# Attention and two expert layers in one kernel: query and key loads moved in the attention's table, and layer 2's token sums in place and operand by operand

## The chip, the core and the metric

The kernel runs on one core of a Trainium2 chip. The core has a matrix engine (PE, with its weight loads shown as PEld), a vector engine (DVE), a scalar engine (ACT), a general one (POOL) and a queue engine (SP) that issues transfers to 16 DMA engines. Each engine takes its instructions in the order of its program and waits on semaphores for the others. The metric is the time of one execution on the device, in microseconds (us); the time given for the kernel before is the median of three runs.

## What is computed

Attention over 4 batches and 12 heads of 448 tokens with 64 numbers each, with queries and keys normalised by their root mean square; then two layers, each up, activation and down, on 1792 tokens of width 768 with 2048 hidden units.

```python
q_n, k_n = (rmsnorm(q, g_q), rmsnorm(k, g_k))
scores = scale * np.matmul(q_n, k_n.transpose(0, 1, 3, 2))
attn = np.exp(scores - max) ; attn = attn / (sum(attn) + 1e-09)
x = (attn @ v) as tokens x 768
h = x @ w_in ;  g = h * (1.0 / (1.0 + np.exp(-h))) ;  y = g @ w_out      # layer 1
h = y @ w_in2 ; g = np.maximum(h, 0.0) ** 2 ;         out = g @ w_out2   # layer 2
```

## The kernel before

**Number format.** Products are made of split operands: an upper part (hi) by a cast, L493 or L495, and a lower part (lo) by a subtraction, L502, and three products of parts per product. The four weight matrices come as 64-bit numbers; each unit of a weight (768 or 512 columns of 128 rows) is loaded raw (L846), turned into 32-bit by one ACT pass (L853) and DVE passes (L857, L861, L867, L873), stored for its later uses (L881, "keep", tiles ki, ko, kp, kq), and split (L493, L502). Later uses load it again (L833).

**Attention.** 24 pairs of heads follow one another. Of each pair, SP loads queries and keys (L516, tile qk, a ring of three buffers) and values (L633). ACT squares them (L527), DVE sums, POOL and DVE take the inverse root in small steps, POOL normalises (L589, two operations, after which the qk buffer is free), PE turns the tiles (L601). Then four chunks of scores follow (L654), each with the maximum on DVE (L665), the exponential on ACT (L672), and turning on PE (L681); PE multiplies with the values (L730), and ACT copies the result into xf (L481). The row sums of the exponentials are inverted, stored into DRAM (L709, tile rd) and read back spread over the partitions (L718, tile R, a ring of two). POOL multiplies xf by R (L753, the step "attended"), and the result is stored (L785, "keep_x", x) for the later batches, or split for layer 1 at once.

**Layers.** Layer 1 runs in 8 segments, 2 halves of the tokens by 4 quarters of the hidden units: up products (L954), silu in two steps (ACT L966, DVE L971), split into gg (one buffer), down products (L1008), sums (L1020); its result y is stored in DRAM (L1040). Layer 2 runs in two halves of 8 groups: each product of token blocks and weights in seven products (L1173, Strassen's scheme) instead of eight, so that it needs sums of weight blocks (L1141) and of token blocks, then relu squared (L1203 to L1207), the split into gh and gl, and the down products (L1249) that DVE adds up (L1276) and SP stores at the end of a half (L1290). The token blocks are made in `combine` (L1054 to L1113): per chunk of 128 rows it loads up to four blocks of y (L1074, tile yf, a ring of five), takes differences (L1084, the step "y_sum", function `less`), and splits them into the operands B11, T2, T3, T4 and, in a second group that may be done later, B21, T1, B22 (`put`).

**What sets the order.** All of it is written as steps of a plan (L97 to L357). A list scheduler with nominal durations simulates the five engines and issues each engine's steps in the order that it finds; buffers come from rings (L25), and a ring's next use waits for all users of the buffer. The steps of the attention are fixed (L141): they are taken on their engine in the order of their nominal times, which is the pair's number times 2 x 5.3 plus the entry of the table `nominal` (L50 to L64). Other steps fill the gaps if the plan finds that they fit before the next fixed step. A number of the table is thus an order, not a wait. The second pool of buffers, which holds gg and yf, opens only when the attention's own buffers are done with, the last keep_x among them (`swap_pools`, L1303).

## Time and profile before

| | |
|---|---|
| runs | 1266.6, 1271.03, 1272.84 us; median 1271.03 |
| the profiled execution | 1261.43 us, its span 1259.5 us |
| mean granted clock of PE | 0.987 |
| busy: PE, DVE, ACT, POOL | 1202.9 (96%), 939.1 (75%), 535.2 (42%), 238.9 us (19%) |
| attention | up to some 320 us of the span |
| layer 1 | some 320 to 790 us |
| layer 2, first and second half | some 790 to 1035 us, and to the end |

The span runs from the first to the last instruction; the profiled execution's time is 1.9 us longer. A timeline row gives the start, the duration, the engine, the line, and the tiles as out<-in; in square brackets stands how long the engine was idle ahead of it and what released it. PEclk is PE's granted clock as a share of 2.4 GHz. SPq is SP's queue of transfers.

### The profile page before, as it was taken

What the parts mean: (1) busy time and instruction counts of PE and PEld (TensorE: products, weight loads), DVE (VectorE), ACT (ScalarE), POOL (GpSimd) and SP (SyncE); (2) the same over time, 40 slices, a digit from 0 to 9 for tenths busy, and PEclk for the clock granted to TensorE, in tenths of its full rate; (3) what the DMA queues carried; (4) which work ended last, traced back from release to release, by engine and by line L of the source; (5) the groups of instructions that cost most, each with busy time, mean ns of one, the idle gap of its engine ahead of it and who ended that gap; (6) DMA issues with size and microseconds to landing.
All of it is one profiled execution on the core that took longest, in us unless ns stands there. A gap on an engine that the chain in (4) does not pass through costs nothing. (4 is left out here: it accounts for less than half of the span.)

```text
span 1259.5 us, 19054 instructions
## 1 busy us (share of the span) xinstructions
PE 1202.9 (96%) x6960; PEld 1050.1 (83%) x6960; DVE 939.1 (75%) x1624; ACT 535.2 (42%) x1129; POOL 238.9 (19%) x449
## 2 busy tenths in 40 slices
PE   5998999999999999999999999999999989999998
PEld 3665666666899999899999988899999988999998
DVE  6887978887588986989899878866667882555554
ACT  6887887776243231434333224443222433221111
POOL 6565656551100100101000001011111100000000
PEclk9998989999999999999999998999999999999999
DMA  5444445557565544597877846945555694544444
GB/s 160 81 98 104 83 90 100 87 101 106 159 184 154 172 130 147 166 339 222 242 253 230 253 160 214 346 170 205 219 211 189 231 310 180 173 169 158 138 141 135
DMA packets 134109, 220.75 MB, mean 175 GB/s; under 512 B 31104, under 2 KB 99456, under 8 KB 134016
## 3 DMA queue, kind: packets, MB, share of 16 engines
q1 hardware_dynamic: 134016, 219.54, 57.8%
q8 instruction: 55, 0.90, 0.4%
q14 instruction: 38, 0.31, 0.1%
HBM read 145.88 MB, written 73.62 MB: 174 GB/s over the span
## 5 line engine op out<-in xcount | busy, mean ns | idle before, releaser
L954 PE MATMUL t<-xb,w 128*128 128x448 f32 x1152 | 243.8, 369 | 6.7 <-DVE g L971 6.6
L1008 PE MATMUL s<-gg,w 128*128 128x448 f32 x1152 | 240.1, 365 | 1.3 <-DVE gg L502 1.3
L954 PEld LDWEIGHTS t<-xb,w 128*128 128x128 f32 x1152 | 217.8, 190 | 26.4 <-DVE g L971 8.2
L1008 PEld LDWEIGHTS s<-gg,w 128*128 128x128 f32 x1152 | 216.2, 188 | 19.0 <-DVE gg L502 1.8
L1249 PE MATMUL s<-w,gh 128*128 128x384 f32 x896 | 227.9, 335 | 0.0
L1249 PEld LDWEIGHTS s<-w,gh 128*128 128x128 f32 x896 | 162.4, 188 | 1.9 <-DVE gg L1276 0.3
L1249 PE MATMUL s<-w,gl 128*128 128x384 f32 x448 | 150.5, 336 | 6.0 <-DVE gl L502 5.9
L1276 DVE TENSOR_TENSOR gg<-s,gg 128x384 f32<-128x384 f32 x196 | 107.7, 554 | 55.4 <-PE s L1249 55.1
L672 ACT ACTIVATE E<-s,mx 112x448 f32<-112x448 f32 x192 | 121.1, 645 | 12.9 <-DVE mx L665 11.1
L1189 DVE TENSOR_TENSOR g<-t,g 128x448 f32<-128x448 f32 x96 | 58.2, 620 | 85.7 <-ACT g L481 57.3
L681 PEld LDWEIGHTS t<-ident,E 112*112 112x112 f32 x768 | 76.7, 138 | 52.5 <-ACT E L672 26.1
L681 PE MATMUL t<-ident,E 112*112 112x112 f32 x768 | 102.1, 274 | 15.9 <-ACT E L672 11.5
L665 DVE TENSOR_REDUCE mx<-s 112x1 f32<-112x448 f32 x192 | 110.8, 619 | 8.3 <-PE s L654 6.8
L502 POOL TENSOR_TENSOR w<-W,w 128x768 fp32r<-128x768 f32 (+1 forms) x17 | 29.2, 1716 | 442.7 <-ACT w L493 432.9
L1249 PEld LDWEIGHTS s<-w,gl 128*128 128x128 f32 x448 | 84.1, 188 | 8.2 <-DVE gl L502 8.2
L654 PE MATMUL s<-T 64*112 64x448 f32 x576 | 87.3, 408 | 3.0 <-ACT T L610 3.0
L493 ACT CAST w<-W 128x768 fp32r<-128x768 f32 (+1 forms) x68 | 49.9, 737 | 93.5 <-PE s L1008 46.4
L502 DVE TENSOR_TENSOR w<-W,w 128x768 fp32r<-128x768 f32 (+1 forms) x95 | 87.4, 927 | 2.9 <-ACT w L493 2.3
L730 PE MATMUL pv<-PT,vv 112*64 112x224 f32 x768 | 83.4, 359 | 0.0
L1199 ACT ACTIVATE g<-g 128x448 f32<-128x448 f32 x48 | 27.5, 575 | 118.7 <-DVE g L1189 118.7
L966 ACT ACTIVATE g<-t 128x448 f32<-128x448 f32 x64 | 34.5, 541 | 89.7 <-PE t L954 87.7
L730 PEld LDWEIGHTS pv<-PT,vv 112*64 112x64 f32 x768 | 51.1, 136 | 20.3 <-issue 0.5
(105 smaller groups left out, 1739.6 us busy)
## 6 DMA issues: line engine op xcount, KB each, us to landing
raw<-in_moe_w_in_dram SPq DMA_DIRECT2D x32, 768.0 KB, 8.4
raw<-in_moe_w_out_dram SPq DMA_DIRECT2D x24, 512.0 KB
raw<-in_moe_w_out_dram SPq DMA_DIRECT2D x16, 768.0 KB, 5.9
su<-w SPq DMA_DIRECT2D x16, 768.0 KB, 5.5
w<-su SPq DMA_DIRECT2D x16, 768.0 KB, 6.7
yf<-y SPq DMA_DIRECT2D x48, 224.0 KB, 7.6
ki<-W SPq DMA_DIRECT2D x16, 384.0 KB, 5.0
ko<-W SPq DMA_DIRECT2D x24, 256.0 KB, 4.9
```

The lines of the kernel that those rows point to most:

```text
L493: nc.scalar.copy(o(), a())
L502: kind, when, any_t(n, rate), lambda e: engine(e).tensor_tensor(o(), a(), h(), ALU.subtract),
L654: nc.tensor.matmul(pts[j].ap[:CP, :S], T.ap[r, 0, a, c * CP:(c + 1) * CP], T.ap[r, 1, b_], start=(k_ == 0), stop=(k_ == 2),)
L665: lambda e, pt=pt, mx=mx: nc.vector.tensor_reduce(mx.ap, pt.ap[:CP, :S], AX.X, ALU.max, negate=True),
L672: lambda e, j=j, c=c, pt=pt, mx=mx, E=E: nc.scalar.activation(E.ap[:, j], pt.ap[:CP, :S], AF.Exp, bias=mx.ap, accum_out=sums.ap[:, j, c:c ...
L681: nc.tensor.transpose(pe.ap[:CP, m * CP:(m + 1) * CP], E.ap[:, j, m * CP:(m + 1) * CP], ident.ap)
L730: nc.tensor.matmul(pv.ap[j * D:(j + 1) * D, c2 * CT * CP:(c2 + 1) * CT * CP], vr.ap[:, j * NCH + m, :], pt.ap[:, j * NCH + m].rearrange("p ...
L954: nc.tensor.matmul(pt.ap[:, :S], w_()[:, c, :], x[c // HC].ap[:, a, c % HC, :], start=(c == 0 and n == 0), stop=(c == NC6 - 1 and n == 2),)
L1008: nc.tensor.matmul(pt.ap[:, :S], w_()[:, f, :], gg.ap[:, k, a, f, :], start=(f == 0 and n == 0), stop=(f == HQ - 1 and n == 2),)
L1189: lambda e: nc.vector.tensor_tensor(o.ap, pt.ap[:, :S], a.ap, ALU.add),
L1249: nc.tensor.matmul(pt.ap[:, :NH], g.ap[:, fi, tc_ * P:(tc_ + 1) * P], w_()[:, 0, nh * NH:(nh + 1) * NH], start=(n == 0), stop=(n == 5),)
L1276: lambda e, o=o, pt=pt: nc.vector.tensor_tensor(o(), pt.ap[:, :NH], o(), ALU.add),
```

## The change

Three things are changed. In the table, the loads of queries and keys go from -47.0 to -48.6, the spread of R from 26.7 to 28.6, and attended, keep_x, x_hi and x_lo from 6 x 5.3 to 8 x 5.3 plus the same rest, which is one pair later. Two durations that the planner assumes for turning on PE grow (0.4 to 0.53 and 0.45). In `combine`, sums are written over one of their operands: T3 = B22 - B12 over B22, T2 = T3 + B11 over B11, T4 = B21 - T2 over B21, so three sums per chunk instead of four in the first group (24 L1084 in all instead of 30), the ring yf gets a sixth buffer, and the second group is taken by operand (B21 of three chunks, then T1, then B22) instead of by chunk. The number of y loads, 48, stays.

```diff
-RINGS = {"xb": 4, "yb": 2, "yf": 5, ...
+RINGS = {"xb": 4, "yb": 2, "yf": 6, ...
...
-        "load_qk": -47.0 + 0.5 * j, "load_v": -12.0, ...
+        "load_qk": -48.6 + 0.5 * j, "load_v": -12.0, ...
...
-        "inverse": 3 * T2 + 2.3, "store_r": 3 * T2 + 2.7, "spread": 26.7 + 0.4 * j,
-        "attended": 6 * T2 + 3.3, "keep_x": 6 * T2 + 4.6, "x_hi": 6 * T2 + 4.9, "x_lo": 6 * T2 + 5.2,
+        "inverse": 3 * T2 + 2.3, "store_r": 3 * T2 + 2.7, "spread": 28.6 + 0.4 * j,
+        "attended": 8 * T2 + 3.3, "keep_x": 8 * T2 + 4.6, "x_hi": 8 * T2 + 4.9, "x_lo": 8 * T2 + 5.2,
...
-            step("turn_q", at, pe_t(0.1 * NCH), turn, reads=[n32, ident], writes=[pt])
+            step("turn_q", at, pe_t(0.53), turn, reads=[n32, ident], writes=[pt])
...
-                step("turn_e", at, pe_t(0.1 * NCH), turn, reads=[(E, j), ident], writes=[pe])
+                step("turn_e", at, pe_t(0.45), turn, reads=[(E, j), ident], writes=[pe])
...
         for c in range(HC):
-            less, put = chunk(c, at, ("B11", "B12", "B21", "B22"))
-            less("T3", "B22", "B12")
-            less("B12", "B12", "B11")
+            less, put = chunk(c, at, ("B12", "B22", "B11", "B21"))
             less("B22", "B22", "B12")
-            less("B21", "B21", "B22")
             put("B11", "B11")
-            put("T2", "B22")
-            put("T3", "T3")
+            less("B11", "B22", "B11", ALU.add)
+            put("T2", "B11")
+            put("T3", "B22")
+            less("B21", "B21", "B11")
             put("T4", "B21")
-        for c in range(HC):
-            less, put = chunk(c, later, ("B11", "B12", "B21", "B22"))
-            put("B21", "B21")
-            less("B12", "B12", "B11")
-            put("T1", "B12")
-            put("B22", "B22")
+        for o, names in (("B21", ("B21",)), ("T1", ("B12", "B11")), ("B22", ("B22",))):
+            for c in range(HC):
+                less, put = chunk(c, later, names)
+                if o == "T1":
+                    less("B12", "B12", "B11")
+                put(o, names[0])
```

What the planner makes of it is seen in the order of the instructions. Line numbers behind L1082 are two to three lower in the changed kernel: L1084 becomes L1082, L1173 becomes L1170, L1249 becomes L1246, L1290 becomes L1287.

SP in the attention, the transfers of one pair in the steady part, of the kernel before and then of the changed one:

```order
L718 DMA R<-rd 64x448 x2
L516 DMA qk<-in_q_dram 112x2x256
L516 DMA qk<-in_k_dram 112x2x256
L709 DMA rd<-sum 112x8x1
L633 DMA vv<-in_v_dram 112x2x256
```
```order
L516 DMA qk<-in_q_dram 112x2x256
L516 DMA qk<-in_k_dram 112x2x256
L718 DMA R<-rd 64x448 x2
L709 DMA rd<-sum 112x8x1
L633 DMA vv<-in_v_dram 112x2x256
```

The loads of queries and keys have moved ahead of R, whose issue waits until rd of the pair before has landed. The raw weight loads (L846) and keeps (L881) that stood between the pairs have moved as well: SP's rows have the first of them, after two at the start, at row 41 before and at row 124 now, of 557.

DVE at the change to layer 1's last segment, before and now (g, t: silu; gg: its split; yf, xb, yb: combine):

```order
L1020 SCALAR_TENSOR_TENSOR part_6997<-s_8347,part_6997 128x448
L495 CAST gg_8390<-g_8145 128x448
L502 TENSOR_TENSOR gg_8390<-g_8242,gg_8390 128x448
L1084 TENSOR_TENSOR yf_8400<-yf_8366,yf_6906 128x448
L502 TENSOR_TENSOR gg_8390<-g_8145,gg_8390 128x448
L1084 TENSOR_TENSOR yf_6906<-yf_6906,yf_6890 128x448
L502 TENSOR_TENSOR xb_8344<-yf_8400,xb_8344 128x448
L1084 TENSOR_TENSOR yf_8366<-yf_8366,yf_6906 128x448
L971 SCALAR_TENSOR_TENSOR g_8407<-g_8407,t_8251 128x448
```
```order
L971 SCALAR_TENSOR_TENSOR g_8380<-g_8380,t_8265 128x448
L1020 SCALAR_TENSOR_TENSOR part_7022<-s_8336,part_7022 128x448
L502 TENSOR_TENSOR xb_8391<-yf_6742,xb_8391 128x448
L502 TENSOR_TENSOR xb_8391<-yf_6769,xb_8391 128x448
L502 TENSOR_TENSOR gg_8366<-g_8203,gg_8366 128x448
L502 TENSOR_TENSOR xb_8410<-yf_6750,xb_8410 128x448
L502 TENSOR_TENSOR gg_8366<-g_8294,gg_8366 128x448
L502 TENSOR_TENSOR w_8374<-W_8237,w_8374 128x512
L971 SCALAR_TENSOR_TENSOR g_8434<-g_8434,t_8356 128x448
L971 SCALAR_TENSOR_TENSOR g_8429<-g_8429,t_8304 128x448
L1082 TENSOR_TENSOR yf_8413<-yf_8413,yf_6873 128x448
```

The sums of combine have moved behind silu's second step for the segment's first tiles. On PE the up products L954 at that place go from 27 matmuls to 36 ahead of the segment's down products.

PE in a steady group of layer 2's first half, from the last product of a group to its first down products, before and now (part, yb, xb: token operands; w: weights):

```order
L1173 MATMUL t<-xb,w 128x448 x9
L1173 MATMUL t<-part,w 128x448 x9
L1249 MATMUL s<-w,gh 128x384 x2
L1249 MATMUL s<-w,gl 128x384
L1249 MATMUL s<-w,gh 128x384 x2
```
```order
L1170 MATMUL t<-xb,w 128x448 x9
L1170 MATMUL t<-part,w 128x448 x9
L1170 MATMUL pv<-yb,w 128x448 x9
L1246 MATMUL s<-w,gh 128x384 x2
L1246 MATMUL s<-w,gl 128x384
```

One product of the next group has moved ahead of the first 48 down products; before it stood behind 36 of them. At the change of halves SP's order of before has nine y loads (L1074) between the stores of the first half (L1290); now the loads stand in one block ahead of the stores, all but one.

## Rows read from the trace of the kernel before

**Rows 1.** Windows: from:to, length, busy PE, PEld, DVE, ACT, POOL; PEclk, DMA share, GB/s.

```profile
60.00:300.00 240.00, 227.04 (x1875) 153.69 (x1872) 201.17 (x388) 191.01 (x501) 136.77 (x301) 0.97 0.52 98
300.00:330.00 30.00, 27.73 (x168) 22.45 (x168) 14.08 (x29) 10.57 (x25) 3.43 (x3) 0.94 0.60 101
330.00:400.00 70.00, 67.78 (x334) 62.33 (x333) 56.26 (x95) 26.16 (x44) 2.75 (x2) 1.00 0.59 177
700.00:800.00 100.00, 95.78 (x461) 88.22 (x461) 79.47 (x127) 30.25 (x50) 7.49 (x5) 0.97 0.67 219
800.00:840.00 40.00, 36.48 (x182) 33.62 (x180) 26.23 (x43) 19.14 (x38) 2.42 (x1) 0.96 0.60 217
840.00:1000.00 160.00, 155.22 (x818) 146.69 (x819) 117.16 (x190) 52.46 (x95) 28.65 (x21) 1.00 0.60 219
1000.00:1050.00 50.00, 45.30 (x229) 41.37 (x228) 40.80 (x80) 16.45 (x31) 0.00 (x0) 0.97 0.86 297
```

**Rows 2.** Timeline of PE: two undisturbed half pairs, and one behind a wait.

```profile
99.47 0.98 PE L681 MATMUL t<-ident,E 112*112 112x112 f32 x8
...
105.08 0.98 PE L681 MATMUL t<-ident,E 112*112 112x112 f32 x8
...
120.60 2.03 PE L681 MATMUL t<-ident,E 112*112 112x112 f32 x8 [4.24 <-ACT E L672]
```

**Rows 3.** Timeline of ACT at the same wait.

```profile
118.84 0.63 ACT L527 ACTIVATE sq<-qk 112x512 f32<-112x512 f32 x1 [6.26 <-DMA qk<-in_q_dram]
```

**Rows 4.** Waits of all engines: us in total, times, longest.

```profile
ACT sq L527 <- DMA qk<-in_q_dram: 27.0, 13, 6.3
```

**Rows 5.** Waits of SP's queue, in the same columns.

```profile
SPq L718 <- DMA rd<-sum: 129.3, 21, 11.1
```

**Rows 6.** Timeline of SP's queue in the attention.

```profile
36.47 0.32 SPq L709 DMA_DIRECT2D rd<-sum  x1
...
43.82 1.10 SPq L718 DMA_DIRECT2D R<-rd  x2
...
98.47 0.39 SPq L709 DMA_DIRECT2D rd<-sum  x1
...
109.48 1.09 SPq L718 DMA_DIRECT2D R<-rd  x2
...
110.67 0.53 SPq L516 DMA_DIRECT2D qk<-in_q_dram  x1
```

**Rows 7.** Timeline of POOL: one pair's normalisation.

```profile
99.34 2.05 POOL L589 TENSOR_TENSOR n<-qk,y 112x512 f32<-112x512 f32 x2
```

**Rows 8.** The page's costliest groups: the subtraction that splits weights on DVE.

```profile
L502 DVE TENSOR_TENSOR w<-W,w 128x768 fp32r<-128x768 f32 (+1 forms) x95 | 87.4, 927 | 2.9 <-ACT w L493 2.3
```

**Rows 9.** Timeline of ACT at the attention's end and layer 1's start.

```profile
304.22 0.66 ACT L853 ACTIVATE W<-raw 128x512 f32<-128x512 f32 x1 [4.79 <-issue]
...
337.43 1.50 ACT L493 CAST gg<-g 128x448 fp32r<-128x448 f32 x3 [6.08 <-DMA x<-xf]
```

**Rows 10.** Timeline of PE in the layers.

```profile
758.31 6.35 PE L954 MATMUL t<-xb,w 128*128 128x448 f32 x18 [4.21 <-DVE g L971]
...
840.01 0.45 PE L1249 MATMUL s<-w,gl 128*128 128x384 f32 x1 [1.21 <-DVE gl L502]
```

**Rows 11.** Timeline of DVE in the layers.

```profile
757.11 0.61 DVE L1084 TENSOR_TENSOR yf<-yf 128x448 f32<-128x448 f32 x1
...
837.71 2.25 DVE L502 TENSOR_TENSOR gl<-g,gh 128x448 fp32r<-128x448 f32 x1
...
1041.21 0.40 DVE L495 CAST xb<-yf 128x448 fp32r<-128x448 f32 x1 [1.74 <-DMA yf<-y]
```

**Rows 12.** Timeline of SP's queue at the change of halves.

```profile
1029.76 2.93 SPq L1290 DMA_DIRECT2D out_dram<-gg  x4
...
1034.16 0.39 SPq L1074 DMA_DIRECT2D yf<-y  x1
```

**Rows 13.** The page's list of DMA issues: KB each, median us to landing.

```profile
raw<-in_moe_w_in_dram SPq DMA_DIRECT2D x32, 768.0 KB, 8.4
```

More of the change, by code (lines that the diff above doesn't have):

```diff
@@ L24 @@
 BEFORE = list(range(40, 72))
-RINGS = {"xb": 4, "yb": 2, "yf": 5, "xl": 2, "v": 1, "V": 2, "part": 2, "xf": 6, "raw": 2, "W": 3, "w": 5, "E": 4, "PT": 4, "qk": 3, "T": 2, "n": 3, "vv": 3, "g": 4}
+RINGS = {"xb": 4, "yb": 2, "yf": 6, "xl": 2, "v": 1, "V": 2, "part": 2, "xf": 6, "raw": 2, "W": 3, "w": 5, "E": 4, "PT": 4, "qk": 3, "T": 2, "n": 3, "vv": 3, "g": 4}
 FORMS = ["raw", "word"]
@@ L54, in nominal @@
     return {
-        "load_qk": -47.0 + 0.5 * j, "load_v": -12.0, "squares": -38.0 + 5.75 * j, "sums": -29.5,
+        "load_qk": -48.6 + 0.5 * j, "load_v": -12.0, "squares": -38.0 + 5.75 * j, "sums": -29.5,
         "newton": -24.1 + 0.24 * j, "newton_i": -24.1 + 0.24 * j,
@@ L1076, in chunk, with less @@
                 )
-            def less(o, a, b):
-                if o not in f:
-                    f[o] = sb([P, S], F32, "yf", None, "yp")
+            def less(o, a, b, op=ALU.subtract):
                 o, a, b = f[o], f[a], f[b]
                 step(
-                    "y_sum", at, any_t(S), lambda e: engine(e).tensor_tensor(o.ap, a.ap, b.ap, ALU.subtract),
+                    "y_sum", at, any_t(S), lambda e: engine(e).tensor_tensor(o.ap, a.ap, b.ap, op),
                     reads=[t for t in (a, b) if t is not o], writes=[o],
```

## The prediction

> **What bounds the kernel now.** I read the windows first. From 60 us to 1050 us TensorE (PE) is the engine that nearly never rests, and what it does not use lies in few places: between 60 and 300 us it is busy 227.04 of 240 us, and in the windows at 300, 330, 700, 800, 840 and 1000 us it lacks 2.27, 2.22, 4.22, 3.52, 4.78 and 4.70 us [rows 1]. The column PEclk tells of a second loss: where it is under 1.00, PE worked at half its clock for a while. One row shows how that hangs together: eight transposes take 0.98 us and the same eight after an idle time of 4.24 us take 2.03 us [rows 2]; 2.03 is the level of 1.2 GHz, 0.98 that of 2.4 GHz. So each window's loss is its idle time plus (1 - PEclk) of its length. That gives, in us: attention (60 to 300) 13.0 + 7.2 = 20.2; its tail (300 to 330) 2.3 + 1.8 = 4.1; layer 1's start (330 to 400) 2.2; layer 1's last change of segment (700 to 800) 4.2 + 3.0 = 7.2; layer 2's start (800 to 840) 3.5 + 1.6 = 5.1; the rest of its first half (840 to 1000) 4.8; its change of halves (1000 to 1050) 4.7 + 1.5 = 6.2. Together 49.8 us: an edit that leaves PE's own work alone can win no more here, and this one leaves it alone.
>
> Then I asked what ends each loss. In the attention PE's wait is for an exponential on ScalarE (ACT), and ACT has stood before it at the square of a query tile, 6.26 us until the load of queries landed [rows 3]; such waits are 27.0 us in 13 places [rows 4]. The load was late because SP, the one queue that issues all transfers, stood at L718: 129.3 us in 21 waits for the store of the row sums, rd, to land [rows 5]. An undisturbed half pair takes PE 5.61 us (99.47 to 105.08), a pair 11.2 [rows 2]; SP went from one rd issue through the wait to R at 109.48 and the queries at 110.67 [rows 6], over 12 us after the issue of rd at 98.47. SP, not PE, sets the pace for some pairs.
>
> **Attention: the load ahead of R.** The change puts the query and key loads ahead of L718's wait. What they then wait for is a free buffer: three pairs share the ring, and the load at 110.67, of the pair three later, could have gone once the normalisation begun at 99.34 on GpSimd (POOL), two operations of 2.05 us together, had ended, at 101.4 [rows 7]. That is 9.3 us earlier, more than the longest wait of ACT, 6.26 us. What is late next is SP's own round: rd's issue to R's issue was 7.35 us where nothing new stood directly ahead of rd (36.47 to 43.82) and 11.0 us at 98.47, with queries and keys right ahead of rd and a weight load and a keep between [rows 6]. In the new order queries and keys follow rd and R, not the other way round, so I am nearest to the first row: 7.35 + 1.10 for R + some 0.4 for rd is 8.9 us, under PE's 11.2. With the second row it is 12.5 and SP still paces (a rival, below). Queued behind the new wait on SP are R, the next rd and the values. R's user, the multiplication L753, comes one pair later than before on POOL, so it has 11.2 us more. R's ring of two then frees that much later too, at about the time at which rd lands; I price this at nothing, with one us a pair if it is late. I leave 2.5 us of the 20.2, ends 0 and 20.2. Gain 17.7.
>
> The Trainium skill (DMA: Bandwidth & Descriptors, section Queues, rings and completion order) says that on each DMA engine the descriptors of SP's row of rings are consumed in the order of their issue. By that, rd pays for transfers issued ahead of it and not for those behind, which is the first row's side; were it otherwise, the sum would be that of the first rival. The two rows agree with it but do not prove it, since more than the loads differs between them.
>
> **Weights leave the attention.** In SP's new order the first weight after the two initial ones is loaded only near the attention's end; before, six units were prepared by then on VectorE (DVE). Some four units move into 300 to 400 us. A unit is about five DVE passes at the 0.93 us of its subtraction [rows 8], so 4.6 us, and four are 18.6 us; DVE has 15.9 idle us between 300 and 330 us and 13.7 in the next 70 [rows 1]. The cover is there, just. If it fails, PE waits for weights. The tail's stall stays in kind: ACT's read of a freshly loaded weight (4.79 us) stood in front of exponentials [rows 9], and the new order has two such reads there. So the tail keeps its 4.1 (ends 0 and 7). Layer 1's start, 2.2 us, hangs on the last store of the attention's result, for which ACT waits 6.08 us before it may write layer 1's first activations [rows 9]; these stores come a pair later, between keeps of weights: I take 3 us, ends 0 and 8. Together -0.8.
>
> **Six sums fewer, and their place.** Six y_sum of 0.61 us [rows 11] are 3.7 us of DVE, worth nothing by themselves: DVE has idle time in the same windows. Their place counts. At 758.31 PE waits 4.21 us for L971, the second half of silu [rows 10]; DVE ran a sum at 757.11, the third there, directly ahead of it [rows 11]. In the new order L971 of three tiles stands ahead of the first sum, and PE has nine more matmuls in hand at that place. The eighteen at 758.31 took 6.35 us; less the 3.0 that the clock cost in that window it is 3.35, so nine are 1.7 us at full clock. I leave 2.2 of 7.2 (ends 0 and 7.2): gain 5.0.
>
> **Layer 2's start.** Of the 5.1 us, 1.2 end at 840.01 [rows 10] and belong to the next step. The 3.9 left are a wait for the third chunk of one operand, B21, which came chunk by chunk with two others. Now B21's three loads come first. The new operands later in line, T1 and B22, are needed later by PE as well. I leave 2.0 (ends 0 and 4): gain 1.9.
>
> **Down products of the first half.** At 840.01 PE waits 1.21 us for gl, the lower half of the activations [rows 10]; DVE began gl at 837.71 behind two subtractions of weights and was done 2.25 us later [rows 11]. Five such waits make the 1.2 + 4.8 = 6.0. In the new order one product of the next group, nine matmuls, stands between the last product and the first down product: the 1.7 us worked out above, if a product's matmul is as long as layer 1's of the same shape. DVE has a third subtraction (0.93) ahead of gl. 1.7 - 0.9 covers 0.8 of the 1.2, so 0.4 five times stays: I leave 2.0 (ends 0 and 6), gain 4.0.
>
> **Change of halves.** DVE waits 1.74 us for a y load at 1041.21 [rows 11]; on SP it stood behind four stores of the result from 1029.76 to 1032.69, and its issue came only at 1034.16 or later [rows 12]. In the new order all but one load stand ahead of the stores. The sixth yf buffer lets them. That makes a burst where the DMA share is already 0.86 [rows 1], and weights of the second half stand among them. I leave 2.2 of 6.2 (ends 0 and 7): gain 4.0.
>
> **The sum.** 17.7 - 0.8 + 5.0 + 1.9 + 4.0 + 4.0 = 31.8 us. The profiled execution took 1261.4 us, so 1229.6 us of its kind. The runs shown lie 5.2 to 11.4 us above it, their median 1271.03 by 9.6. Such a spread fits waits that vary with landing times, of which the change takes the most; I add 4 us, not 9.6, and forecast **1233 us**.
>
> **The rivals.** *SP still paces the attention.* If rd goes on landing 11 us after its issue, SP's round is 12.5 us against 11.2, and twenty pairs give back what was to be won: 17.7 us, 1229.6 + 17.7 + 4 = 1251 us. For it: 21 waits with 129.3 us are 6.2 us each even after SP's other work [rows 5]. Against it: that row has weight traffic inside, which goes. Chance 0.15.
>
> *Layer 2's reordering only moves its waits.* Operand by operand T1 and B22 arrive later than chunk by chunk; if PE then waits there as long as before, 1.9 + 4.0 + 4.0 are lost: 1229.6 + 9.9 + 4 = 1243 us. For it: the DMA share of 0.86 at the change of halves. Against it: it is 0.60 in the other windows of layer 2's first half [rows 1], where two of the three waits lie. Chance 0.17.
>
> *Weights starve layer 1, and the kernel is slower.* If the idle 29.6 us of DVE can't be used, since the weights come only as fast as two load buffers turn round (8.4 us from issue to landing [rows 13]), PE waits before each of some ten units of the first segments: the 18.6 us of moved work, and after each wait a stretch at half clock, which cost 1.8 us after the one stall of the tail and 3.0 after the one at 758.31 [rows 1, 10], so up to 30 us. 1229.6 + 48.6 + 4 = 1282 us. It turns the sign once it costs the 31.8 us of the sum, from seven of the ten units on; fewer stay on the faster side. For it: SP's new order has no such load between rows 9 and 124. Against it: in 330 to 400 us PE lost only 2.22 while weights were loaded and prepared there too. Chance 0.05.
>
> *The loads do not move in time.* Their lead could be eaten by the wait for the buffer, if POOL frees it late, and the layers' gains by the rivals above: 1271 us. Against it: the 9.3 us between 101.4 and 110.67 [rows 6, 7]. Chance 0.05.
>
> **Chances.** The forecast has 0.58. Those at 1243 and 1251 are faster too: 0.58 + 0.17 + 0.15 = 0.90, less a little for several misses at once, 0.88. A measurement can tell about 0.5%, 6.4 us; within it 0.07, slower 0.05. The range reaches from all 49.8 us won without an addition, 1212, to the first rival with the full 9.6 added, 1257; beyond it lie some 0.14.
>
> **What would show it.** Right: SP's waits at L718 under 60 us in all, no wait of ACT at L527 over 1 us between 60 and 300 us, PEclk 1.00 there, PE starts 5.61 us apart throughout; no PE wait for gl at the first down product; under 2.5 us of PE idle at the two changes in the layers. Wrong: PE waits for w in 330 to 400 us; L753 or R on SP's list of waits for POOL; a DVE wait for yf over 2 us at the second half's start; squares still waiting for qk.

## The result

The changed kernel takes 1222.24 us (median of four runs, 1220.61 to 1225.05); four runs of the kernel before beside it have the median 1268.92 us. The ratio is 0.963, with a 95% interval of 0.960 to 0.967: faster by 3.7%. The forecast was 1233 us and 1212 to 1257.

The profiled execution took 1222.14 us, its span 1220.2 us, 39.3 us less than before. The same windows as in [rows 1], of the changed kernel:

```profile
60.00:300.00 240.00, 236.08 (x1988) 163.51 (x1985) 205.95 (x391) 197.73 (x516) 130.95 (x302) 0.99 0.56 88
300.00:330.00 30.00, 24.04 (x107) 21.45 (x106) 19.56 (x36) 9.50 (x17) 2.85 (x2) 0.89 0.77 183
330.00:400.00 70.00, 70.00 (x347) 64.88 (x347) 64.25 (x106) 27.75 (x46) 1.79 (x1) 1.00 0.66 194
700.00:800.00 100.00, 98.20 (x487) 90.37 (x486) 76.39 (x127) 37.17 (x67) 9.22 (x7) 1.00 0.72 250
800.00:840.00 40.00, 40.00 (x218) 38.53 (x217) 23.16 (x39) 15.93 (x29) 3.23 (x3) 1.00 0.43 151
840.00:1000.00 160.00, 160.00 (x857) 153.44 (x856) 121.36 (x210) 60.57 (x107) 34.17 (x24) 1.00 0.69 247
1000.00:1050.00 50.00, 49.93 (x269) 47.72 (x268) 20.73 (x38) 16.56 (x32) 1.16 (x1) 1.00 0.52 188
```

Two columns tell it: busy PE (the third number) and PEclk (the last but two). In the attention's window PE went from 227.04 to 236.08 of 240 us and PEclk from 0.97 to 0.99. In 840 to 1000 us, where five waits for gl were, PE is busy all 160.00 us. One window got worse: 300 to 330 us has 24.04 busy us where it had 27.73, at a PEclk of 0.89. The stages lie earlier now, so a window of after doesn't hold quite the work of the same window of before; the starts of the stages say it exactly. Here they are for all kernels of this study, each read from the first matmul of a stage in PE's timeline (in us; up: start of layer 1's first up product, 2.6 to 2.8 us ahead of the end of the attention's last work on PE, 4.1 in e8, and so a measure of the attention's length; layer 1: from there to layer 2's first product; first half: from there to the start of the last product of its eighth group; change: from there to the start of the same product of the next group).

| kernel | up | layer 1 | first half | change | span | ratio to before (95%) |
|---|---|---|---|---|---|---|
| before | 312.3 | 478.9 | 218.9 | 32.9 | 1259.5 | 1 |
| changed | 293.0 | 475.3 | 209.9 | 27.6 | 1220.2 | 0.963 (0.960-0.967) |
| e1 table only | 289.4 | 483.7 | 218.7 | 33.1 | 1240.1 | 0.985 (0.980-0.989) |
| e2 combine only | 309.4 | 472.3 | 209.9 | 27.6 | 1233.3 | 0.982 (0.976-0.988) |
| e3 loads and attended | 287.4 | 489.7 | 218.6 | 32.9 | 1244.7 | 0.986 (0.982-0.991) |
| e4 turning times | 307.4 | 487.3 | 218.9 | 33.2 | 1261.8 | 0.996 (0.994-0.999) |
| e5 loads alone | 297.8 | 489.2 | 218.6 | 33.0 | 1253.6 | 0.995 (0.992-0.998) |
| e6 rd in 112 pieces | 287.0 | 475.3 | 218.5 | 32.9 | 1229.4 | 0.978 (0.974-0.982) |
| e7 changed, old turning times | 287.0 | 476.5 | 209.9 | 27.6 | 1215.0 | 0.967 (0.963-0.971) |
| e8 sums in place | 306.6 | 478.9 | 211.2 | 27.9 | 1240.2 | 0.990 (0.988-0.993) |
| e9 rd in 224 pieces | 287.0 | 482.1 | 218.9 | 33.1 | 1236.2 | 0.984 (0.978-0.990) |
| e10 combine, rd in 224 pieces | 286.9 | 469.8 | 210.3 | 27.6 | 1208.5 | 0.961 (0.954-0.967) |
| e11 changed, rd in 224 pieces | 287.0 | 466.1 | 210.3 | 28.9 | 1206.1 | 0.961 (0.955-0.966) |
| e12 by operand | 304.3 | 479.2 | 214.9 | 29.3 | 1242.7 | 0.988 (0.982-0.994) |

So the 39.3 us of span come from the attention (19.3), layer 1 (3.6), layer 2's first half (9.0), its change of halves (5.3) and some 2 us behind it. The runs of the kernel before differ from one group of runs to the next (medians 1257.0 to 1268.9 us), so ratios are always to the runs made beside a kernel. The stages come from one execution each. Layer 1's scatter is large: e6 and e9 have the same order there, yet take 475.3 and 482.1 us, and the whole difference is PE's busy time for the same matmuls (242.7 and 240.0 us for up and down products against 246.0 and 243.5 us on their pages). So up to some 7 us in that column are no reading by themselves. Also, where the second group of operands is taken by operand, layer 2's first product stands ahead of the last 24 matmuls of layer 1 and not of the last 12; some 2.4 us of layer 1's 3.6 thus belong to the first half.

What is late next in the changed kernel stands in PE's timeline, all its waits of 0.75 us or more after 60 us, and the first up product:

```profile
280.11 1.21 PE L681 MATMUL t<-ident,E 112*112 112x112 f32 x8 [3.19 <-ACT E L672]
...
293.03 0.88 PE L954 MATMUL t<-xb,w 128*128 128x448 f32 x3
...
317.96 7.36 PE L954 MATMUL t<-xb,w 128*128 128x448 f32 x25 [5.96 <-DVE g L971]
...
758.22 10.30 PE L1008 MATMUL s<-gg,w 128*128 128x448 f32 x48 [0.78 <-DVE g L1020]
...
787.10 2.06 PE L1170 MATMUL t<-yb,w 128*128 128x448 f32 x9 [0.96 <-ACT w L493]
```

ACT's timeline says what the first two waits (280.11 and 317.96) come from:

```profile
278.56 0.89 ACT L853 ACTIVATE W<-raw 128x768 f32<-128x768 f32 x1 [5.17 <-DMA raw<-in_moe_w_in_dram]
...
313.81 0.66 ACT L853 ACTIVATE W<-raw 128x512 f32<-128x512 f32 x1 [8.18 <-DMA raw<-in_moe_w_out_dram]
```

At 280.11 the exponentials, and at 317.96 layer 1's silu, stood on ACT behind the reading of a raw weight that had not landed. These are weights that the old order had loaded among the pairs. The first is not new in kind: the kernel before had such a stall at the attention's end, behind the read of [rows 9] at 304.22:

```profile
305.55 1.56 PE L681 MATMUL t<-ident,E 112*112 112x112 f32 x8 [2.25 <-ACT E L672]
```

The second is: before, layer 1's start hung on the store of the attention's result [rows 9].

### The profile page after: what moved, and what is told of

Read it like the earlier page. It is cut to its first block, busy times and chain, and to the rows that moved or that the text cites. A ratio compares the mean times of both kernels' runs of the same rounds, so it can differ in the third digit from the quotient of the medians.

```text
span 1220.2 us, 19070 instructions
## 1 busy us (share of the span) xinstructions
PE 1187.6 (97%) x6960; PEld 1045.2 (86%) x6960; DVE 917.9 (75%) x1596; ACT 547.2 (45%) x1141; POOL 248.9 (20%) x459
## 4 chain that ended last, share of the span: by engine, by line
PE 87%; DMA 6%; DVE 4%; ACT 1%; issue 1%; POOL 1%; SPq 0%; ACTq 0%; DVEq 0%
PE s L1008 18%; PE s L1246 17%; PE t L954 17%; PE t L1170 11%; PE t L681 6%; PE pv L730 6%; PE s L654 6%; PE pv L1170 4%; PE t L601 2%; DMA yf<-y 2%; DMA raw<-in_moe_w_out_dram 1%; DMA raw<-in_moe_w_in_dram 1%; DMA rd<-sum 1%; DMA w<-su 1%; DMA su<-w 1%
## 5 line engine op out<-in xcount | busy, mean ns | idle before, releaser
L954 PE MATMUL t<-xb,w 128*128 128x448 f32 x1152 | 242.2, 368 | 6.7 <-DVE g L971 6.7
L1008 PE MATMUL s<-gg,w 128*128 128x448 f32 x1152 | 239.5, 365 | 0.8 <-DVE g L1020 0.8
L954 PEld LDWEIGHTS t<-xb,w 128*128 128x128 f32 x1152 | 217.6, 189 | 25.9 <-DVE g L971 8.1
L1008 PEld LDWEIGHTS s<-gg,w 128*128 128x128 f32 x1152 | 216.2, 188 | 18.6 <-DVE g L1020 1.1
L1246 PE MATMUL s<-w,gh 128*128 128x384 f32 x896 | 227.6, 334 | 0.1
L1246 PEld LDWEIGHTS s<-w,gh 128*128 128x128 f32 x896 | 162.0, 188 | 1.5 <-DMA w<-su 0.4
L1246 PE MATMUL s<-w,gl 128*128 128x384 f32 x448 | 149.7, 334 | 0.0
L681 PEld LDWEIGHTS t<-ident,E 112*112 112x112 f32 x768 | 74.3, 135 | 37.5 <-ACT E L672 19.3
L681 PE MATMUL t<-ident,E 112*112 112x112 f32 x768 | 96.1, 268 | 4.8 <-ACT E L672 4.1
L502 DVE TENSOR_TENSOR w<-W,w 128x768 fp32r<-128x768 f32 (+1 forms) x97 | 83.8, 871 | 3.1 <-ACT w L493 2.4
L1246 PEld LDWEIGHTS s<-w,gl 128*128 128x128 f32 x448 | 84.1, 188 | 0.0
L502 POOL TENSOR_TENSOR w<-W,w 128x512 fp32r<-128x512 f32 (+1 forms) x15 | 24.1, 1604 | 279.2 <-ACT w L493 207.4
L502 POOL TENSOR_TENSOR gl<-g,gh 128x448 fp32r<-128x448 f32 x12 | 14.7, 1223 | 266.2 <-DVE gh L495 198.9
```

The costliest lines, as they stand in the source:

```text
L502: kind, when, any_t(n, rate), lambda e: engine(e).tensor_tensor(o(), a(), h(), ALU.subtract),
L681: nc.tensor.transpose(pe.ap[:CP, m * CP:(m + 1) * CP], E.ap[:, j, m * CP:(m + 1) * CP], ident.ap)
L954: nc.tensor.matmul(pt.ap[:, :S], w_()[:, c, :], x[c // HC].ap[:, a, c % HC, :], start=(c == 0 and n == 0), stop=(c == NC6 - 1 and n == 2),)
L1008: nc.tensor.matmul(pt.ap[:, :S], w_()[:, f, :], gg.ap[:, k, a, f, :], start=(f == 0 and n == 0), stop=(f == HQ - 1 and n == 2),)
L1246: nc.tensor.matmul(pt.ap[:, :NH], g.ap[:, fi, tc_ * P:(tc_ + 1) * P], w_()[:, 0, nh * NH:(nh + 1) * NH], start=(n == 0), stop=(n == 5),)
```

## Where the attention's gain comes from

In the changed kernel ACT hardly waits for queries any more, 3.7 us against the 27.0 of [rows 4], and what is left lies ahead of 23 us:

```profile
ACT sq L527 <- DMA qk<-in_q_dram: 3.7, 3, 1.6
```

SP still waits for rd, 77.0 us against the 129.3 of [rows 5], and now also for POOL's normalisation to free a qk buffer:

```profile
SPq L718 <- DMA rd<-sum: 77.0, 21, 6.7
...
SPq L516 <- POOL n L589: 64.4, 16, 5.1
```

The prediction had two candidates for what makes the queries late: their place behind L718's wait, or the weight traffic among the pairs. The change takes both away, so two runs take away one each, and two more run the change's halves.

**e1, the table's part alone.** The diff is that of the table and the two turning times, ahead of the prediction.

> The kernel before with the whole table change (loads, attended one pair later, assumed turning times) and the old combine. If the two parts of the change are independent, the first up product comes at about 293 us as in the changed kernel (312.3 before) and the layers keep their old losses at the last change of segment, layer 2's start and change of halves and the five gl waits; the new wait of about 6 us at layer 1's start comes with it. Sum: 1269 - 19.3 + 7 = about 1257 us. The rival, that the parts need each other (the combine's gain is that of a shifted plan), gives either less than 8 us or more than 30 us of gain here.

Measured: 1241.82 us against 1263.87 beside it, 22.0 us faster, more than the 12 expected. The first up product is at 289.4 us, and layer 2 keeps its old lengths to 0.2 us. Layer 1 is 4.8 us longer; its start has a wait of 4.37 us. The attention won more than in the changed kernel, though both issue it in the same order; there a raw weight landed later.

**e2, the combine's part alone.** `combine`'s diff and the ring of six.

> The kernel before with the new combine and the sixth yf buffer only. Attention as before: the first up product at 312 us within 3, 13 waits of ACT for query loads. Layer 2 from its first product to the end takes 447 us as in the changed kernel (463 before), the 4.2-us wait at the last change of segment goes: 1269 - 16 - 7 = about 1246 us. If the layers' gain came from the table instead, no change: 1266 to 1270 us.

Measured: 1236.79 us against 1263.87, 27 us by the medians and 23 by the ratio, 0.982. Layer 2's two stages have exactly the lengths of the changed kernel, 209.9 and 27.6 us. The two halves together, 1.5% and 1.8%, make 3.4%; the change as a whole has 3.7%, from 3.4 to 4.0. Within the intervals they add up, and neither needs the other. (By the spans of single executions 19.4 and 26.2 us would make 45.6, where the whole has 39.3.)

**e3, loads, spread and attended moved, weights left among the pairs.**

```diff
-    "load_qk": -47.0      "spread": 26.7      "attended", "keep_x", "x_hi", "x_lo": 6 * T2 ...
+    "load_qk": -48.6      "spread": 28.6      "attended", "keep_x", "x_hi", "x_lo": 8 * T2 ...
```

> The kernel before with the table's loads, spread and attended moved, but with the old assumed turning times: the query and key loads stand ahead of R, while weight loads and keeps stay among the pairs. Theory one (the order on SP behind the wait for rd is what makes queries late): waits of ACT for queries under 6 us in all instead of 27, attention shorter by 15 to 19 us, about 1251 us. Rival (weight traffic on SP, ACT and DVE among the pairs is what makes them late): the attention is not shorter by more than 5 us, 1264 us or more.

Measured: 1245.29 us, ratio 0.986. The window of the attention and ACT's wait for queries:

```profile
60.00:300.00 240.00, 238.92 (x2011) 166.37 (x2011) 211.82 (x407) 202.43 (x525) 142.91 (x306) 1.00 0.64 105
```

```profile
ACT sq L527 <- DMA qk<-in_q_dram: 3.6, 3, 1.9
```

PE is busy 238.92 of 240 us at full clock, with the weights still there: the attention is 25 us shorter. Some of it is given back at layer 1's start, in PE's timeline:

```profile
301.24 16.69 PE L954 MATMUL t<-xb,w 128*128 128x448 f32 x81 [2.32 <-DVE g L971]
322.34 2.23 PE L1008 MATMUL s<-gg,w 128*128 128x448 f32 x5 [4.41 <-ACT gg L493]
```

**e4, the assumed turning times alone, which take the weights out and leave R first.**

```diff
-    step("turn_q", at, pe_t(0.1 * NCH), ...)     step("turn_e", at, pe_t(0.1 * NCH), ...)
+    step("turn_q", at, pe_t(0.53), ...)          step("turn_e", at, pe_t(0.45), ...)
```

> The kernel before with the two assumed turning times alone, which take the weight preparation out of the attention and leave R ahead of the queries on SP. Theory one: the late queries stay, ACT still waits over 15 us for them, attention shorter by at most 5 us, 1264 us or more (with up to 7 us more lost at layer 1's start). Rival (weight traffic): attention shorter by some 18 us, about 1251 us plus up to 7 at layer 1's start.

Measured: 1257.65 us, ratio 0.996. The same two views:

```profile
60.00:300.00 240.00, 228.80 (x1894) 154.98 (x1894) 191.45 (x371) 189.43 (x501) 127.45 (x301) 0.98 0.46 82
```

```profile
ACT sq L527 <- DMA qk<-in_q_dram: 27.9, 11, 5.0
```

ACT waits 27.9 us for queries, as before. So the weights among the pairs were not the cause, and the order on SP was. The turning times by themselves shorten the attention by 4.9 us and lengthen layer 1 by 8.4.

**e5, the loads and the spread without attended.** The prediction priced attended's move as mere cover.

> The kernel before with the loads and the spread moved in the table, but attended and what follows it left where they were, and the old turning times. It tells whether the place of the loads alone does it or whether POOL, which waits for R in front of the next normalisation (53.4 us in 13 waits before), matters as much. Theory one: ACT's waits for queries under 8 us, attention ends within 4 us of that with attended moved too (287 us against 312), 16 to 19 us faster. Rival: R is now issued later, POOL waits longer for it ahead of the normalisation that frees the queries' buffer, so SP waits for POOL and the attention wins under 10 us.

Measured: 1255.19 us, ratio 0.995. ACT's waits for queries are gone here too (2.8 us), yet the attention ends at 297.8 us, 10.4 later than with attended moved as well. The rows of one such place, on POOL, then ACT, then PE:

```profile
126.64 1.31 POOL L753 TENSOR_TENSOR xf<-xf,R 128x448 f32<-128x448 f32 x1 [3.31 <-DMA R<-rd]
```

```profile
127.98 0.56 ACT L493 CAST xb<-xf 128x448 fp32r<-128x448 f32 x1 [4.47 <-POOL xf L753]
```

```profile
129.23 0.59 PE L681 MATMUL t<-ident,E 112*112 112x112 f32 x4 [1.73 <-ACT E L672]
```

POOL waits 3.31 us for R at L753; ACT waits 4.47 us for that product, since the upper part of x for layer 1 stands in its order ahead of the next exponentials; PE waits for those. It is the same wait for rd, reaching PE by another way. Moving the loads opens one way and moving attended the other. The loads alone win 14.5 of the 24.9 us by which e3 shortens the attention; by the ratio they win 0.5% where both win 1.4%. Attended alone was not run.

## What makes rd late

The prediction held that rd lands late because query and key loads stand directly ahead of it in the queue. In the changed kernel they do not, and SP's timeline shows rd hardly quicker:

```profile
105.67 0.93 SPq L709 DMA_DIRECT2D rd<-sum  x1
106.70 0.50 SPq L633 DMA_DIRECT2D vv<-in_v_dram  x1
110.68 0.31 SPq L516 DMA_DIRECT2D qk<-in_q_dram  x1
111.04 0.45 SPq L516 DMA_DIRECT2D qk<-in_k_dram  x1
115.14 1.09 SPq L718 DMA_DIRECT2D R<-rd  x2
```

From the issue of rd to that of R are 9.5 us here, with the queries behind rd. Over all 24 pairs of SP's timeline the median is 9.9 us (7.6 to 12.4), where the kernel before has 10.1 (7.4 to 13.1). The order is not quite without effect: the medians are 9.4 to 10.1 us in the kernels with the loads behind R (before, e2, e4, e8, e12) and 8.2 to 9.9 in those with the loads ahead (changed, e1, e3, e5, e7), so about a microsecond. The page's list of DMA issues says the same with 9.6 us to landing against 10.1, but in these two kernels the trace tells the landing of only 5 of the 24 stores (columns: KB of one, median us to landing; the q1 row: packets, MB, share of 16 engines' span):

```profile
rd<-sum SPq DMA_DIRECT2D x24, 3.5 KB, 9.6
```

```profile
q1 hardware_dynamic: 134016, 219.54, 57.8%
...
rd<-sum SPq DMA_DIRECT2D x24, 3.5 KB, 10.1
```

What else is odd about rd: its 3.5 KB go out as single numbers, since the tile has a token chunk's sums side by side where DRAM has a chunk's tokens side by side. Run e6 stores them as the tile has them.

**e6, rd in 112 pieces of 32 bytes.**

```diff
-    rd.ap.rearrange("j c p -> p (j c)"), sums.ap.rearrange("p j c -> p (j c)")
+    rd.ap.rearrange("j c p -> (j c p)").rearrange("(p x) -> p x", x=2 * NCH), sums.ap.rearrange("p j c -> p (j c)")
```

> The kernel before with rd stored as 112 rows of 8 numbers instead of 896 single numbers scattered; R then holds the inverse sums in a wrong order, so the division of the attention's result is wrong, and nothing else changes in the order on the engines. It takes away the wait at L718 instead of moving the loads past it. If rd is late because of its own 896 small pieces, it lands in under 4 us (5.2 median, 10.9 at most before by tile), SP's waits at L718 fall from 129 us to under 60, ACT's waits for queries from 27 to under 8, and the attention is 15 to 20 us shorter. If rd is late because query and key loads stand ahead of it in the queue, as the prediction had it, its landing and all else stays within 20%.

Measured: 1233.24 us against 1260.81, ratio 0.978.

```profile
q1 hardware_dynamic: 115200, 219.54, 54.5%
...
rd<-sum SPq DMA_DIRECT2D x24, 3.5 KB, 1.4
```

```profile
60.00:300.00 240.00, 240.00 (x2020) 167.81 (x2017) 213.44 (x411) 201.85 (x524) 143.60 (x305) 1.00 0.37 111
```

18,816 packets fewer are 24 times 784, which is 896 less 112: rd had gone out as 896 packets a pair. It now lands in 1.4 us (median of all 24), though queries and keys stand ahead of it as before. PE is busy 240.00 of 240 us at full clock, without one move of a load. The share of the DMA engines falls from 0.52 [rows 1] to 0.37, while what they move rises from 98 to 111 GB/s.

**e9, the same with the result kept: 224 pieces of 16 bytes.** Each partition holds four neighbouring tokens' sums, so DRAM takes them so, and the multiplication reads R with a stride.

```diff
-        rd = dram([2, NCH, CP], "rd", 3)
+        rd = dram([2, CP, NCH], "rd", 3)
...
-                rd.ap.rearrange("j c p -> p (j c)"), sums.ap.rearrange("p j c -> p (j c)")),
+                rd.ap.rearrange("j p c -> p j c"), sums.ap),
...
-                    rd.ap[j].rearrange("c p -> (c p)").unsqueeze(0).to_broadcast([D, S])),
+                    rd.ap[j].rearrange("p c -> (p c)").unsqueeze(0).to_broadcast([D, S])),
...
-            lambda e: engine(e).tensor_tensor(t.ap, t.ap, R.ap, ALU.mult),
+            lambda e: engine(e).tensor_tensor(
+                t.ap.rearrange("d (c p) -> d c p", c=NCH), t.ap.rearrange("d (c p) -> d c p", c=NCH),
+                R.ap.rearrange("d (p c) -> d c p", c=NCH), ALU.mult),
```

> The kernel before with rd laid out so that each partition's four inverse sums of a head lie side by side: 224 pieces of 16 bytes instead of 896 of 4, R read back in that order, and the multiplication L753 on POOL reading R with a stride. Order on all engines unchanged, result unchanged. If the number of pieces is what makes rd late, it lands between the 1.4 us of 112 pieces and the 10.1 us of 896, about 3 to 4 us; the attention ends at about 288 us (312 before, 287 with 112 pieces) with the query loads still behind R, about 1240 to 1245 of 1263 us. If it lands after 6 us or more, the attention keeps over half of its loss. L753 may take longer than 1.15 us with the stride.

Measured: 1235.84 us against 1257.02, ratio 0.984; the attention ends at 287.0 us.

```profile
q1 hardware_dynamic: 117888, 219.54, 54.3%
...
rd<-sum SPq DMA_DIRECT2D x24, 3.5 KB, 2.9
```

```profile
60.00:300.00 240.00, 240.00 (x2015) 167.65 (x2014) 213.85 (x411) 200.86 (x523) 144.70 (x303) 1.00 0.39 111
```

Landing takes 2.9 us (median of all 24). The number of the pieces, their size and their spread over DRAM change together in e6 and e9, so which of the three sets the price isn't told apart. The Trainium skill (DMA: Bandwidth & Descriptors, section Rules for kernel authors) says that a last dimension which isn't contiguous becomes one descriptor per element and is best rearranged; the packet counts here agree with it, 896 for 896 numbers. The price of the strided read stands in the row of L753 (minimum, median, maximum in ns), of before and of this run:

```profile
L753 POOL TENSOR_TENSOR xf<-xf,R x24: 1131/1152/2427, 53.7 to 332.7; 128x448 f32<-128x448 f32 x24
```

```profile
L753 POOL TENSOR_TENSOR xf<-xf,R x24: 1362/1382/1399, 53.4 to 300.4; 128x448 f32<-128x448 f32 x24
```

That is 0.23 us a pair on POOL, which is busy 144.70 of 240 us in the window above.

## The change with and without the cause

**e10, combine's change with rd in 224 pieces, the table as before.**

> No change in the table: the new combine and the sixth yf buffer, with rd in 224 pieces as in the run above. If the waits for rd were all that the table change cures, this beats the changed kernel: attention ends at 288 us, layer 1 has no wait at its start since the attention's last stores are not moved and the weights stay prepared early, layer 2 as in the changed kernel: span 288 + 469 + 447 = about 1204 us against 1220, ratio to before 0.952 to 0.958.

**e11, the whole change with rd in 224 pieces.**

> The changed kernel with rd in 224 pieces. If the loads ahead of R already hide rd's landing, little is left to win: the 77.0 us of SP's waits at L718 fall, the time stays within 4 us of the changed kernel's, ratio 0.960 to 0.966. If rd's slow pieces also slow the raw weights at layer 1's start (waits of ACT up to 8.2 us there), some 3 to 6 us more are won.

Measured: 1207.07 us for e10 and 1207.22 us for e11, against 1257.02 beside them; ratios 0.961 and 0.961. The two are equal within their intervals: with rd quick the table's move wins nothing that the store's layout doesn't. e10 lies just outside the ratio expected of it (0.952 to 0.958); e11's ratio is the expected one, but its time is 15 us under the changed kernel's and not within 4. Windows of e11, from the attention over layer 1's start:

```profile
60.00:300.00 240.00, 240.00 (x2018) 167.81 (x2015) 211.03 (x399) 201.00 (x521) 138.45 (x303) 1.00 0.34 96
300.00:330.00 30.00, 30.00 (x149) 27.81 (x149) 27.47 (x51) 13.34 (x23) 1.53 (x1) 1.00 0.66 210
330.00:400.00 70.00, 70.00 (x347) 64.87 (x347) 63.89 (x103) 25.59 (x40) 1.78 (x1) 1.00 0.64 195
```

PE never waits there; in the changed kernel the second of these had 24.04 of 30 us and a clock of 0.89. The raw weights that PE waited for at 280.11 and 317.96 came late because of rd's pieces as well. One of them SP issues at the same moment in the changed kernel and in e11 (whose numbering is two higher here). In the changed kernel ACT waits for it until 278.56; in e11 ACT reads it at 273.28 without a wait. The rows of SP in the changed kernel, SP in e11 and ACT in e11:

```profile
266.83 0.40 SPq L846 DMA_DIRECT2D raw<-in_moe_w_in_dram  x1
```

```profile
266.84 0.40 SPq L848 DMA_DIRECT2D raw<-in_moe_w_in_dram  x1
```

```profile
273.28 0.93 ACT L855 ACTIVATE W<-raw 128x768 f32<-128x768 f32 x1
```

So it is the landing that got quicker and not the issue, and rd's layout, with L753's read of it, is all that differs between the two kernels. e10, whose weights stay among the pairs, has none of these waits either:

```profile
300.00:330.00 30.00, 30.00 (x150) 27.81 (x149) 25.26 (x42) 12.97 (x22) 1.59 (x1) 1.00 0.59 174
```

By spans e11 is 14.1 us ahead of the changed kernel. By ratios, 0.961 (0.955 to 0.966) against 0.963 (0.960 to 0.967), the two can't be told apart, since the kernel before was itself quicker in the group of e11. Their own runs don't overlap, 1205.3 to 1208.2 against 1220.6 to 1225.1 us, but were not made side by side. That e11 is better is thus likely, not settled.

**e7, the changed kernel with the old turning times.**

> The changed kernel without the two assumed turning times: loads, attended and combine as changed, weights prepared among the pairs as before. Attention ends at about 287 us (293 in the changed kernel), layer 1 loses two waits of 2.3 and 4.4 us at its start instead of one of 6.0. Time within 4 us of the changed kernel, ratio to before 0.960 to 0.966. If the weights in the attention did harm, the attention would be longer than 293 us and the ratio over 0.968.

Measured: 1219.19 us against 1260.81, ratio 0.967 (0.963 to 0.971). The attention ends at 287.0 us; layer 1's start has waits of 1.86 and 2.50 us in place of 5.96. Its span is 5.2 us under the changed kernel's, and the ratios, 0.967 (0.963 to 0.971) and 0.963 (0.960 to 0.967), overlap: the turning times bring no gain that can be seen.

**e8, sums in place only, and e12, by operand only**, each with six yf buffers.

> The kernel before with the sums in place and the sixth yf buffer, but the second group of operands chunk by chunk as before. If the place of the loads by operand gives the gain at layer 2's start, PE waits there as before, now for B21 or another third chunk, over 2 us. If the six sums fewer and the new plan do it, the last change of segment, the gl waits and the change of halves are cured as with both (some 23 to 27 us faster in all). I expect the change of segment and halves cured, layer 2's start not, 20 us faster.

> The kernel before with the second group of operands taken by operand and the sixth yf buffer, the four sums per chunk left as they were. With the in-place run it splits the combine's gain. I expect layer 2's start cured (no wait over 1 us for a third chunk, against 2.8 us with in-place sums alone), the last change of segment not cured (about 4 us waiting for L971, since a fourth sum stands there), the gl waits gone because the plan places a product there, as with in-place sums; 10 to 18 us faster than before.

Measured: e8 1247.80 us, ratio 0.990 (0.988 to 0.993), so 12.5 us and not 20; e12 1241.97 us, ratio 0.988. PE's rows at the last change of segment and layer 2's start, of e8:

```profile
754.37 3.90 PE L954 MATMUL t<-xb,w 128*128 128x448 f32 x18 [0.48 <-DVE g L971]
...
799.33 0.68 PE L1170 MATMUL t<-xb,w 128*128 128x448 f32 x2 [2.79 <-DVE xb L495]
```

and at layer 2's start and the first gl wait, of e12:

```profile
803.69 1.89 PE L1173 MATMUL t<-yb,w 128*128 128x448 f32 x8 [2.17 <-DVE w L502]
807.19 2.08 PE L1173 MATMUL pv<-yb,w 128*128 128x448 f32 x9 [1.62 <-ACT g L1199]
...
841.25 0.45 PE L1249 MATMUL s<-w,gl 128*128 128x384 f32 x1 [1.53 <-DVE gl L502]
```

e8 went as expected in its places, if not in its total: the change of segment has 0.48 us left of 4.21, layer 2's start keeps 2.79 us, no wait for gl is left. e12's total, 15 us by the ratio, lies within the 10 to 18 expected, but its places were a miss on most counts. Layer 2's start keeps 2.17 and 1.62 us; they are for a weight and for activations and not for a third chunk, but the start isn't cured. Two waits for gl remain where the kernel before had five, 1.53 us at 841.25 and this one:

```profile
1002.24 0.44 PE L1249 MATMUL s<-w,gl 128*128 128x384 f32 x1 [1.48 <-DVE gl L502]
```

The change of segment, expected to stay, is cured there as well, with 1.03 us left. On DVE four sums still stand ahead of silu's L971; the last of them and L971:

```profile
753.97 0.62 DVE L1084 TENSOR_TENSOR yf<-yf 128x448 f32<-128x448 f32 x1
...
755.99 0.62 DVE L971 SCALAR_TENSOR_TENSOR g<-g,t 128x448 f32<-128x448 f32 x1 [0.57 <-ACT g L966]
```

On PE, six down products (L1008) stand there between the up products, in e8 too, where the kernel before had none. Both parts together give 209.9 us for the first half, each alone 211.2 and 214.9. What the two have in common is the sixth yf buffer, and it wasn't run by itself; which of the new plan's places it accounts for stays open.

## Why the prediction was right, and where not

- **Losses and their places.** 49.8 us were counted as all that could be won; the span fell by 39.3. All places named in [rows 1] moved, and PE's idle time nowhere else by more than 2 us. But the count is no upper bound: e11, which leaves PE's own work alone too, has a span 53.4 us under that of before. The count left out 1.6 us of idle PE from 400 to 700 us; the rest stays open, and layer 1's scatter is of that size.
- **Attention.** Gain predicted 17.7 us, measured 19.3, the tail included. The step "the load ahead of R" is right: e3 and e5 against e4 show that SP's order decides whether queries are late. The 25.3 us by which e6 and e9 end the attention earlier (312.3 to 287.0) are all that there was to win.
- **Why rd is late.** This step fails. It took 7.35 us (nothing new directly ahead) for rd's time in the new order, and 11.0 us as the effect of queries ahead. Over the 24 pairs it is 9.9 us with no queries directly ahead, and in 112 pieces rd lands in 1.4 us with queries right ahead: the pieces make it late, and the place in the queue adds about a microsecond. SP's waits at L718 are 77.0 us and not under 60. That the attention's gain came out all the same is luck as far as this step goes: 9.9 us from rd to R and 1.1 for R leave 0.2 of PE's 11.2 us a pair, where the sum had 8.9 and so 2.3 to spare. The rival at 1251 us was nearer than its chance of 0.15 said.
- **Attended.** Priced at nothing, as cover for R. It was worth 10.4 us of the attention: e5 without it keeps that much of the loss, by way of POOL and ACT.
- **Weights out of the attention.** Predicted -0.8 us for the tail and layer 1's start together; it is some -8. The tail was to keep its 4.1 us and has 3.2 of idle time and some 1.8 of clock at 280.11 (PEclk 0.89 from 278 to 294 us), which the 19.3 us of the attention already contain; its mechanism (ACT stands at a raw weight ahead of the exponentials) is the one named. Layer 1's start was to go from 2.2 us to 3. The window at 300 us now loses 6.0 + 3.3 = 9.3, that at 330 nothing, so this term was mis-sized by some six us. Its wait is also another than the one named: not the last store of the attention's result but a raw weight, for which ACT stood 8.18 us ahead of silu. The slower rival, weights starving layer 1, began here and ended after one wait.
- **Last change of segment.** Gain predicted 5.0 us; of 7.2 some 0.8 is left (758.22), so 6.4. But the step named the sums' place as the reason, and e12 has nearly the same cure with four sums ahead of L971, with six down products on PE in between. The sums' place is thus not the only way to it; how much it does in the changed kernel stays open.
- **Layer 2's first half.** Predicted 1.9 + 4.0, measured 9.0. The two us left for gl were too many: the product placed ahead of the down products covers the wait wholly, 160.00 of 160 us, third subtraction or not.
- **Change of halves.** Predicted 4.0, measured 5.3 and up to 2 behind it; the stores no longer stand ahead of the loads, and 49.93 of 50 us are busy.
- **From the profiled execution to the runs.** 4 us were added; the changed kernel's median lies 0.1 us from its profiled execution. The spread of the runs goes with the waits: from the lowest to the highest run it is 8 to 17 us in the kernels that keep the attention's waits in whole or in part (before, e2, e4, e5, e8, e12; 6.2 for the four runs of before beside the result) and 3 to 7 us in the others. These 3.9 us and the 7.5 by which the sum was short (31.8 for 39.3), less 0.6 of rounding, are the 10.8 between forecast and result. The sum came so near because its errors went both ways: the weights' term was some seven us too good, the layers' other terms and the attention's too small.

## What to carry to other kernels

When an in-order queue waits for a small transfer, look at the number of its pieces before its place in the queue: here a new layout of 3.5 KB undoes the whole attention loss that a reordering of 24 pairs' loads undoes almost. A reordering that hides a wait can hide it on one way and leave another; follow every engine that waits for the same tile. And what goes out of a busy stage comes in at the next: ask what its loads will meet there.

## What the runs showed of the hardware

A store of 896 single 4-byte numbers took some 10.1 us beside the attention's other loads (the page's median, of five stores, and the median over all 24 pairs from its issue to that of the load that waits for it); 224 pieces of 16 bytes took 2.9 us, 112 pieces of 32 bytes 1.4 us, of the same 3.5 KB. The 896 pieces also slowed others: the DMA engines' share in the attention fell from 0.52 to 0.39 and 0.37 while their rate rose from 98 to 111 GB/s, and a raw weight issued at the same moment was read 5 us earlier (273.28 against 278.56). By the packet records between 60 and 300 us the 4-byte packets hold only 0.05 of the share themselves; the rest is that others got shorter, 1024-byte packets from 71 ns on average before (112 in the changed kernel) to 57 in e6. POOL's multiplication of 128 x 448 numbers took 1.15 us with contiguous operands and 1.38 us with one read at a stride of four.
